# Alternating halves of up and down projections in an MoE layer, and the high part of keys and queries a round ahead of the low part, on one core

## The chip, the core and the metric

The kernel runs on one core of a Trainium2 chip. The metric is the device time of one execution in microseconds (us). The kernel before takes 898.13 us, the median of three runs (897.16 to 899.61). The profile is of one further execution, of 898.34 us.

The engines are TensorE (PE; its weight loads are PEld), VectorE (DVE), ScalarE (ACT), GpSimd (POOL) and SyncE (SP, which only issues DMAs here). Each works through its own queue of instructions in order, and waits on semaphores for the others.

## What is computed

Attention with soft-capped scores, then a first MoE layer (one expert, no routing), then a second one with a normalised gate. Tensors are float32; the weights arrive as float64.

```python
# attention: batch 4, 12 heads, 448 tokens, 64 per head
scores = cap * tanh(q @ k.T / sqrt(64) / cap)          # cap = 30
attn = softmax(scores)                                  # over the keys
x = (attn @ v)                                          # -> 1792 tokens x 768
# first MoE layer, 768 -> 2048 -> 768
h = x @ w_in
x = (h - tanh(h)) @ w_out
# second MoE layer, 768 -> 1024 -> 768
h = x @ w_in2
e = exp(h - max(h))
solu = h * e / (sum(e) + 1e-9)
out = (layernorm(solu) * g_ln) @ w_out2
```

## The kernel before

The 1792 tokens are worked on in two halves (`hb` 0 and 1), one after the other: attention, first MoE layer, second MoE layer for the first half, and then the same for the second half. A half of 896 tokens has 12 pairs of heads.

Products are computed to nearly full float32: every operand is split into a high part in the matmul's float format (`...h`) and the rest (`...l`), and one product is three matmuls, high x high, high x low and low x high. The splitting is work for VectorE and ScalarE. The float64 weights are taken apart on VectorE as well (lines L111 to L113 turn the words `st` into a float32 `f`, L120 makes the low part `w`); the second half reads most of them back as saved, split tiles.

**Attention.** The order of the work is written by hand: the loop over rounds in `attention` issues in each round one step of each of several pairs, and every engine keeps that order. `load(p)` fetches keys and queries of pair p (`kq`, three buffers, mostly by GpSimd's queue), `split_qk(p)` makes `kqh` by a cast and `kql` by a subtraction on VectorE (L290, L291, two buffers each), `scores(p)` (L308 into the PSUM tile `s`, L314 into `x`), `tanh(p)` and the exponential on ScalarE, `values(p)` (L340 into `o`), and on VectorE the sums `sm` (L362, L363) and the copies `ou` (L382) and `su` (L387), which release the PSUM buffers that `o`, `so` and `x` share.

**The tiles' memory.** SBUF tiles come from pools by stage. In the attention `kqh` and `kql` are in one pool, their buffers one behind the other. A pool of the next stage stands on memory that a pool of the stage before had, and a tile's first writer waits for the last user of that memory. So the second attention's tiles stand on those of the first half's second MoE layer, whose last output tiles `ot` (three, each 128 x 768) are copied from PSUM (L761, L763, L765) and sent to `out` by SyncE (L766).

**First MoE layer.** The 2048 hidden columns come in four chunks (`NCHUNK` = 4) of four tiles of 128. `up(c, half)` computes two hidden tiles of a chunk into the PSUM tiles `hp` (L500 to L502; tag "a", two buffers), and `nonlinear` makes g = h - tanh h of each, by ScalarE and by VectorE's L534 (`gf`), L537 (`t`), L538, L539, and splits it into `gh` and `gl` (L543; six buffers each, a chunk needs four). `down(c)` goes over the six output tiles d = 0 to 5: each is a product over the chunk's four hidden tiles into the PSUM tile `op` (L556 to L558; tag "b", two buffers), which is then added to the accumulator `acc` in SBUF (L563, VectorE; for chunk 0 a copy by ScalarE). An up or down tile has 896 columns, worked on as blocks of 512 and 384; `turned()` alternates which comes first. Here the scheduler orders each engine's instructions from the program's order and its estimates.

What decides the order around the change are these lines, in which a chunk's up tiles come before the down tiles of the chunk ahead of it:

```python
        for c in range(NCHUNK):
            if c + 1 < NCHUNK:
                up(c + 1, 0)
                up(c + 1, 1)
            down(c)
```

Of the kernel before, what the change touches and what calls it, by code (L numbers as in the profile page):

```python
# [10 lines left out]
F32R = mybir.dt.float32r  # L11
# [18 lines left out]
def fused_kernel(ctx, tc, qk_in, v, cap, w1, w2, w3, w4, gln, out):  # L30
    nc = tc.nc
    B, H, S, D = 4, 12, 448, 64
    DM = H * D
    P = 128
# [4 lines left out]
    NK = DM // P  # L39
# [6 lines left out]
    KW = qk_in.shape[3] - S  # L46
    KQ0 = KW - 128

    NCHUNK = w2.shape[0] // NK
# [31 lines left out]
    def caps(part):  # L81
        if part == 0:
            nc.vector.reciprocal(tscale, capt)
            nc.vector.tensor_scalar_mul(tscale, tscale, 1.0 / math.sqrt(D))
            return
        nc.vector.scalar_tensor_tensor(ncap, capt, -1.0, capt, ALU.mult, ALU.min)
        nc.vector.tensor_scalar(shift, ncap, 64.0, 0.0, ALU.add, ALU.min)
        nc.vector.scalar_tensor_tensor(guard, ncap, math.log(1e-9), shift, ALU.add, ALU.add)
# [117 lines left out]
    def load_w1(c, half):  # L206
        ts = []
        for i in range(NK // 2):
            ts += cols(unit(f"1_{c}_{half}_{i}", w1u[(c * 2 + half) * (NK // 2) + i], 2), 2)
        return ts  # L210
# [51 lines left out]
    def attention(ap, hb, xh, xl, rest=None):  # L262
        pairs = [(bb, j) for bb in range(HB) for j in range(NP)]
        n = len(pairs)
        raw, qk, vs, sc, ts, os_, so, fin, rss, rds, rbs, sm = ({} for _ in range(12))
# [13 lines left out]
        def load_v(p):  # L279
# [2 lines left out]
            (nc.sync if hb == 0 and p < 2 else nc.gpsimd).dma_start(vf, v[HB * hb + bb, j])  # L282
            vs[p] = vf

        def split_qk(p):
            kq = raw.pop(p)
            h = ap.tile([P, KW + S], F32R, tag="kqh", name="kqh")
            l = ap.tile([P, KW + S], F32R, tag="kql", name="kql")
            for cs in (slice(KQ0, KW + S), slice(0, KQ0)) if hb == 0 and p == 0 else (slice(0, KW + S),):
                nc.vector.tensor_copy(h[:, cs], kq[:, cs])  # L290
                nc.vector.tensor_tensor(l[:, cs], kq[:, cs], h[:, cs].bitcast(F32), ALU.subtract)  # L291
            qk[p] = (h, l)
            if hb == 0 and p == 0:
                caps(0)
            if hb == 0 and p == 1:
                caps(1)
# [133 lines left out]
        def at(p, fn, *a, m=n):  # L430
            if 0 <= p < m:
                fn(p, *a)
# [3 lines left out]
        for i in range(-5, n):  # L436
            e = i + 2
            at(i, values)
            at(i + 1, tanh)
            at(i, sums_added if hb else sums)  # L440
            at(i - 2, finish1)
            at(i - 3, finish2)
            at(i - 5, finish3)
            at(i + 3, split_qk)
            at(i, evict_v)
            if hb:
                at(i, evict_s, m=n - 1)
            at(i + 2, scores)
            at(i + 1, exp)
            if hb:  # L450
                at(i + 1, presum)
            if hb == 0 and i == 0:
                nc.scalar.activation(gcol, guard, AF.Exp)
            if rest and i == -1:
                rest[2]()
            if not hb:
                at(i, evict_s, m=n - 1)
            at(e - 2, mid, m=WA)
            at(i + 5, load)
            at(e, fetch, m=WA)  # L460
            at(i + 3, load_v)
            at(e - 3, low, m=WA)
            at(e - 1, high, m=WA)
# [16 lines left out]
    def moe1(mp, hb, xh, xl, yh, yl):  # L480
        acc = [mp.tile([P, HT], F32, tag=f"acc{d}", name=f"acc{d}", bufs=1) for d in range(NK)]
        gs = {}
        place.update(pool=(mp, WX1), at=-1)

        blocks = [(0, 512), (512, HT)]

        def turned():
            blocks.reverse()
            return list(blocks)

        def flat(ps):
            return ps.rearrange("p a b -> p (a b)")

        def up_mms(hp, wt, m, k0, k1, gg=None):
            ms = slice(m * P, (m + 1) * P)
            parts = [(flat(hp)[:, a:b], slice(a, b)) for a, b in turned()] if gg is None else [(hp[:, g, :S], slice(g * S, (g + 1) * S)) for g in gg]
            for o, cs in parts:
                for kk in range(k0, k1):
                    wh, wl = wt[kk]
                    nc.tensor.matmul(o, wh[:, ms], xh[kk][:, cs], start=(kk == 0), stop=False)  # L500
                    nc.tensor.matmul(o, wh[:, ms], xl[kk][:, cs], start=False, stop=False)  # L501
                    nc.tensor.matmul(o, wl[:, ms], xh[kk][:, cs], start=False, stop=(kk == NK - 1))  # L502

        def first():

            gs[0] = []
            wts = [load_w1(0, 0), load_w1(0, 1)]
            hps = [pst("hp", "ab"[half]) for half in range(2) for _ in range(2)]
            for g, k0, k1 in ((0, 0, NK), (1, 0, 3), (1, 3, 4), (1, 4, 5), (1, 5, 6)):
                for m in range(3):  # L510
                    up_mms(hps[m], wts[m // 2], m % 2, k0, k1, (g,))
                    if k1 == NK and g == 1:
                        nonlinear(0, hps[m])
            up_mms(hps[3], wts[1], 1, 0, NK)
            nonlinear(0, hps[3], True)

        def up(c, half):
            gs.setdefault(c, [])
            wt = load_w1(c, half)
            for m in range(2):  # L520
                hp = pst("hp", "a")
                up_mms(hp, wt, m, 0, NK)
                nonlinear(c, hp, True)

        def nonlinear(c, hp, whole=False):
            h = flat(hp)[:, :HT].rearrange("p (a b) -> p a b", a=2) if whole else hp[:, :, :S]
            u = mp.tile([P, 2, S], F32, tag="u", name="u")
            nc.scalar.activation(u, h, AF.Square)  # L528
            t = mp.tile([P, 2, S], F32, tag="t", name="t")
            nc.scalar.activation(t, h, AF.Tanh)  # L530
            mk = mp.tile([P, 2, S], U8, tag="mk", name="mk")
            nc.scalar.activation(mk, t, AF.Square, scale=TS)
            gf = mp.tile([P, 2, S], F32, tag="gf", name="gf")
            nc.vector.scalar_tensor_tensor(gf, u, C2, h, ALU.mult, ALU.mult)  # L534
            w = mp.tile([P, 2, S], F32, tag="w", name="w", bufs=1)
            nc.scalar.activation(w, u, AF.Square, bias=gat)
            nc.vector.tensor_tensor(t, h, t, ALU.subtract)  # L537
            nc.vector.scalar_tensor_tensor(gf, w, GB, gf, ALU.add, ALU.mult)  # L538
            nc.vector.copy_predicated(gf, mk, t)  # L539
            gh = mp.tile([P, 2, S], F32R, tag="gh", name="gh", bufs=6)  # L540
            gl = mp.tile([P, 2, S], F32R, tag="gl", name="gl", bufs=6)
            nc.scalar.copy(gh, gf)
            nc.vector.tensor_tensor(gl, gf, gh.bitcast(F32), ALU.subtract)  # L543
            gs[c].append((gh, gl))

        def down(c):
            for d in range(NK):
                wt = load_w2(c, d)
                op = pst("op")
                nm = CH // P  # L550
                fo = flat(op)
                for a, b in turned():
                    for m in range(nm):
                        gh, gl = (flat(g)[:, a:b] for g in gs[c][m])
                        wh, wl = wt[m]
                        nc.tensor.matmul(fo[:, a:b], wh, gh, start=(m == 0), stop=False)  # L556
                        nc.tensor.matmul(fo[:, a:b], wh, gl, start=False, stop=False)  # L557
                        nc.tensor.matmul(fo[:, a:b], wl, gh, start=False, stop=(m == nm - 1))  # L558
                a = acc[d]
                if c == 0:  # L560
                    nc.scalar.copy(a, fo[:, :HT])
                else:
                    nc.vector.tensor_tensor(a, fo[:, :HT], a, ALU.add)  # L563
                if c == NCHUNK - 1:
                    nc.scalar.copy(yh[d], a)
                    nc.vector.tensor_tensor(yl[d], a, yh[d].bitcast(F32), ALU.subtract)

        first()
        if hb:
            for _ in range(3):  # L570
                held = sp.tile([P, 512, 2], U32, tag="st", name="held", bufs=3)
                nc.vector.tensor_copy(held[:, 0, :1].bitcast(F32), flat(gs[0][3][1])[:, :1].bitcast(F32))
        for c in range(NCHUNK):
            if c + 1 < NCHUNK:
                up(c + 1, 0)
                up(c + 1, 1)
            down(c)
            if hb and c < NK // 2:
                sums_w3(c)

# [316 lines left out]
```

## Time and profile before

| | |
|---|---|
| median of three runs | 898.13 us (897.16 to 899.61) |
| profiled execution | 898.34 us |
| its span (first to last instruction) | 896.6 us |
| mean granted TensorE clock | 0.998 |
| TensorE busy | 886.3 us, 99% |
| VectorE busy | 700.7 us, 78% |
| ScalarE busy | 431.7 us, 48% |
| bytes moved | 150.83 MB |

Busy time is the time in which an engine had an instruction under way; matmuls overlap, so that a busy TensorE can still be one that is held up between two of them, or that runs at a lower clock. The granted clock says which share of TensorE's full 2.4 GHz the chip gave it in a stretch. Waits are idle times of an engine by what ended them. In a row, L500 is the kernel's line, `hp<-xh,w` the tile written and those read, and x4 the number of instructions that a row stands for.

### The profile page before, as it was taken

To read this page: it belongs to the slowest core of one execution; us is meant where nothing else is said; L and a number is where in the kernel's file an instruction comes from. 1 tells how busy PE (TensorE), PEld (TensorE's weight loads), DVE (VectorE), ACT (ScalarE), POOL (GpSimd) and SP (SyncE) were. 2 spreads that over 40 slices of the span, in tenths; PEclk is the share of its full clock that TensorE was granted. 3 is DMA by queue.
4 is the path that set the end of the run, shared out by engine and by line. 5 is a ranking of instruction groups with operands and counts; after the bars stand their busy time and mean duration, and the time that the engine had idled before them with its cause. 6 is when DMAs were issued, how large, how long until landed. Compare 5 with 4: busy or idle time off the path is not lost.

```text
span 896.6 us, 13069 instructions
## 1 busy us (share of the span) xinstructions
PE 886.3 (99%) x5135; PEld 709.5 (79%) x5135; DVE 700.7 (78%) x1071; ACT 431.7 (48%) x483; POOL 49.0 (5%) x88
## 2 busy tenths in 40 slices
PE   9999999999999999999999999999999999999998
PEld 5444699888989888888874447989899989887887
DVE  6687889989999892788437997796999874679851
ACT  7999367446154231443158990763642621222311
POOL 2211000000000000001022210000000000000100
PEclk9999999999999999999999999999999999999999
DMA  8554690675643874631155732356765542266101
GB/s 293 185 183 144 215 350 24 224 250 183 191 138 121 283 246 156 228 138 47 53 200 198 221 128 88 118 179 215 238 213 196 173 148 75 93 211 223 68 36 53
DMA packets 48584, 150.83 MB, mean 168 GB/s; under 512 B 10700, under 2 KB 13772, under 8 KB 48524
## 3 DMA queue, kind: packets, MB, share of 16 engines
q1 hardware_dynamic: 41340, 120.81, 40.4%
q0 software_dynamic: 7040, 29.20, 9.4%
q8 instruction: 40, 0.66, 0.3%
q14 instruction: 20, 0.16, 0.0%
q10 hardware_dynamic: 144, 0.00, 0.0%
HBM read 109.65 MB, written 40.19 MB: 167 GB/s over the span
## 4 chain that ended last, share of the span: by engine, by line
PE 61%; DVE 5%; DMA 1%; ACT 1%; issue 1%; SPq 0%; DVEq 0%
PE op L557 5%; PE op L558 5%; PE op L556 5%; PE hp L500 4%; PE hp L502 4%; PE hp L501 4%; PE hp L258 4%; PE hp L259 4%; PE hp L260 4%; PE oab L755 2%; PE oab L759 2%; PE oab L756 2%; PE o L340 2%; PE s L308 2%; PE tp L609 1%; PE oab L757 1%
## 5 line engine op out<-in xcount | busy, mean ns | idle before, releaser
L500 PE MATMUL hp<-xh,w 128*128 128x512 f32 (+2 forms) x384 | 140.2, 366 | 2.1 <-DVE t L537 2.1
L501 PE MATMUL hp<-xl,w 128*128 128x512 f32 (+2 forms) x384 | 140.3, 365 | 0.0
L502 PE MATMUL hp<-xh,w 128*128 128x512 f32 (+2 forms) x384 | 140.2, 365 | 0.0
L557 PE MATMUL op<-gl,w 128*128 128x512 f32 (+1 forms) x336 | 122.2, 364 | 1.1 <-DVE gl L543 1.0
L558 PE MATMUL op<-gh,w 128*128 128x512 f32 (+1 forms) x336 | 122.2, 364 | 0.0
L556 PE MATMUL op<-gh,w 128*128 128x512 f32 (+1 forms) x336 | 121.7, 362 | 0.0
L119 ACT CAST w<-f 128x512 fp32r<-128x512 f32 x60 | 37.3, 622 | 117.0 <-DVE f L113 95.3
L500 PEld LDWEIGHTS hp<-xh,w 128*128 128x128 f32 x384 | 72.4, 189 | 12.1 <-issue 3.7
L502 PEld LDWEIGHTS hp<-xh,w 128*128 128x128 f32 x384 | 72.5, 189 | 8.1 <-issue 0.7
L501 PEld LDWEIGHTS hp<-xl,w 128*128 128x128 f32 x384 | 72.5, 189 | 8.1 <-issue 0.7
L340 PE MATMUL o<-t,vf 128*32 128x448 f32 x768 | 77.8, 542 | 0.0
L332 ACT ACTIVATE t<-t,shift,capt 128x3136 f32<-128x3136 f32 (+2 forms) x26 | 72.8, 2807 | 0.7
L557 PEld LDWEIGHTS op<-gl,w 128*128 128x128 f32 x336 | 63.1, 188 | 9.0 <-DVE gl L543 1.9
L556 PEld LDWEIGHTS op<-gh,w 128*128 128x128 f32 x336 | 63.1, 188 | 7.1
L558 PEld LDWEIGHTS op<-gh,w 128*128 128x128 f32 x336 | 63.0, 188 | 6.5
L325 ACT ACTIVATE t<-s,tscale 128x1344 f32<-128x1344 f32 x48 | 63.5, 1380 | 5.6 <-PE s L308 5.6
L113 DVE SCALAR_TENSOR_TENSOR f<-st,f 128x512 uint32<-128x512 uint32 x90 | 61.5, 688 | 1.1
L112 DVE SCALAR_TENSOR_TENSOR f<-st,f 128x512 uint32<-128x512 uint32 x90 | 61.3, 688 | 0.9
L340 PEld LDWEIGHTS o<-t,vf 128*32 128x32 f32 x768 | 22.7, 109 | 43.4 <-issue 38.7
L563 DVE TENSOR_TENSOR acc<-op,acc 128x896 f32<-128x896 f32 x36 | 39.1, 1087 | 19.7 <-PE op L558 19.7
L528 ACT ACTIVATE u<-hp 128x896 f32<-128x896 f32 x32 | 29.5, 921 | 50.8 <-PE hp L502 50.8
L259 PE MATMUL hp<-w,xh 128*128 128x512 f32 x123 | 48.0, 390 | 0.0
(184 smaller groups left out, 1815.6 us busy)
## 6 DMA issues: line engine op xcount, KB each, us to landing
st<-in_moe_w_out_dram SPq DMA_DIRECT2D x53, 512.0 KB
d<-w SPq DMA_DIRECT2D x53, 512.0 KB
w<-d SPq DMA_DIRECT2D x37, 512.0 KB
st<-in_moe_w_in_dram SPq DMA_DIRECT2D x25, 512.0 KB
kq<-in_qk_dram POOLq DMA_DIRECT2D x21, 480.0 KB, 4.1
w<-d POOLq DMA_DIRECT2D x13, 512.0 KB, 4.9
rw<-d SPq DMA_DIRECT2D x12, 512.0 KB
dT<-tw SPq DMA_DIRECT2D x12, 512.0 KB
```

Of the source, the lines that this page charges most:

```text
L112: nc.vector.scalar_tensor_tensor(f, st[:, :, 1], 0xC0000000, f, ALU.bitwise_and, ALU.bitwise_or)
L113: nc.vector.scalar_tensor_tensor(f, st[:, :, 0], 29, f, ALU.logical_shift_right, ALU.bitwise_or)
L259: nc.tensor.matmul(ps, sh, ml, start=False, stop=False)
L325: nc.scalar.activation(t[:, 3 * half:3 * half + 3], s[half][:, :, :S], AF.Tanh, scale=tscale)
L332: nc.scalar.activation(t[:, sl], t[:, sl], AF.Exp, bias=shift, scale=capt)
L340: nc.tensor.matmul(o[cs, :S], vf[:, r, cs], t[:, 6 if r == 3 else 2 * r + g // 2], start=(r == 0), stop=(r == 3))
L500: nc.tensor.matmul(o, wh[:, ms], xh[kk][:, cs], start=(kk == 0), stop=False)
L501: nc.tensor.matmul(o, wh[:, ms], xl[kk][:, cs], start=False, stop=False)
L502: nc.tensor.matmul(o, wl[:, ms], xh[kk][:, cs], start=False, stop=(kk == NK - 1))
L556: nc.tensor.matmul(fo[:, a:b], wh, gh, start=(m == 0), stop=False)
L557: nc.tensor.matmul(fo[:, a:b], wh, gl, start=False, stop=False)
L558: nc.tensor.matmul(fo[:, a:b], wl, gh, start=False, stop=(m == nm - 1))
```

## The change

Three things are moved; no operation is added or left out.

- **Up and down alternate.** For chunks 1 and 2 the order is now: first half of the next chunk's up tiles, three down tiles of this chunk, second half of the up tiles, the other three down tiles. Chunk 0 and the last chunk keep their order. It holds for both token halves.
- **Two down tiles go over the hidden tiles outermost.** In the last down tile of chunk 2 and the first of chunk 3, the loop over the four hidden tiles is the outer one and the two column blocks the inner one; before, a column block was finished before the next.
- **The high part a round ahead.** In the second attention, `kqh` of a pair is cast one round before its `kql` is subtracted, behind `evict_s` (which issues `su`) in VectorE's order, and `kqh` has three buffers in place of two.

```diff
--- before.py
+++ after.py
@@ -282,12 +282,21 @@
             (nc.sync if hb == 0 and p < 2 else nc.gpsimd).dma_start(vf, v[HB * hb + bb, j])
             vs[p] = vf
 
+        highs = {}
+
+        def high_qk(p):
+            h = highs[p] = ap.tile([P, KW + S], F32R, tag="kqh", name="kqh", bufs=3 if hb else 2)
+            if hb:
+                nc.vector.tensor_copy(h, raw[p])
+            return h
+
         def split_qk(p):
+            h = highs.pop(p) if hb else high_qk(p)
             kq = raw.pop(p)
-            h = ap.tile([P, KW + S], F32R, tag="kqh", name="kqh")
             l = ap.tile([P, KW + S], F32R, tag="kql", name="kql")
             for cs in (slice(KQ0, KW + S), slice(0, KQ0)) if hb == 0 and p == 0 else (slice(0, KW + S),):
-                nc.vector.tensor_copy(h[:, cs], kq[:, cs])
+                if not hb:
+                    nc.vector.tensor_copy(h[:, cs], kq[:, cs])
                 nc.vector.tensor_tensor(l[:, cs], kq[:, cs], h[:, cs].bitcast(F32), ALU.subtract)
             qk[p] = (h, l)
             if hb == 0 and p == 0:
@@ -445,6 +454,7 @@
             at(i, evict_v)
             if hb:
                 at(i, evict_s, m=n - 1)
+                at(i + 4, high_qk)
             at(i + 2, scores)
             at(i + 1, exp)
             if hb:
@@ -543,19 +553,22 @@
             nc.vector.tensor_tensor(gl, gf, gh.bitcast(F32), ALU.subtract)
             gs[c].append((gh, gl))
 
-        def down(c):
-            for d in range(NK):
+        def down(c, ds=range(NK)):
+            for d in ds:
                 wt = load_w2(c, d)
                 op = pst("op")
                 nm = CH // P
                 fo = flat(op)
-                for a, b in turned():
-                    for m in range(nm):
-                        gh, gl = (flat(g)[:, a:b] for g in gs[c][m])
-                        wh, wl = wt[m]
-                        nc.tensor.matmul(fo[:, a:b], wh, gh, start=(m == 0), stop=False)
-                        nc.tensor.matmul(fo[:, a:b], wh, gl, start=False, stop=False)
-                        nc.tensor.matmul(fo[:, a:b], wl, gh, start=False, stop=(m == nm - 1))
+                bl = turned()
+                parts = [(a, b, m) for a, b in bl for m in range(nm)]
+                if (c, d) in ((NCHUNK - 2, NK - 1), (NCHUNK - 1, 0)):
+                    parts = [(a, b, m) for m in range(nm) for a, b in (bl if m % 2 == 0 else bl[::-1])]
+                for a, b, m in parts:
+                    gh, gl = (flat(g)[:, a:b] for g in gs[c][m])
+                    wh, wl = wt[m]
+                    nc.tensor.matmul(fo[:, a:b], wh, gh, start=(m == 0), stop=False)
+                    nc.tensor.matmul(fo[:, a:b], wh, gl, start=False, stop=False)
+                    nc.tensor.matmul(fo[:, a:b], wl, gh, start=False, stop=(m == nm - 1))
                 a = acc[d]
                 if c == 0:
                     nc.scalar.copy(a, fo[:, :HT])
@@ -571,10 +584,13 @@
                 held = sp.tile([P, 512, 2], U32, tag="st", name="held", bufs=3)
                 nc.vector.tensor_copy(held[:, 0, :1].bitcast(F32), flat(gs[0][3][1])[:, :1].bitcast(F32))
         for c in range(NCHUNK):
-            if c + 1 < NCHUNK:
-                up(c + 1, 0)
-                up(c + 1, 1)
-            down(c)
+            for k in range(2):
+                if c + 1 < NCHUNK:
+                    up(c + 1, k)
+                if c:
+                    down(c, range(k * NK // 2, (k + 1) * NK // 2))
+            if c == 0:
+                down(c)
             if hb and c < NK // 2:
                 sums_w3(c)
```

The order of VectorE in the first half's first MoE layer, where chunk 2's up tiles meet chunk 1's down tiles. `hp_2009` and `hp_2096` are the second and third up tile of chunk 2, `f`, `st` and the `w` of L112 to L120 belong to weights that are being converted. Before:

```order
L534 SCALAR_TENSOR_TENSOR gf_2052<-u_2046,hp_2009 128x896
L113 SCALAR_TENSOR_TENSOR f_2439<-st_2437,f_2439 128x512
L537 TENSOR_TENSOR t_2048<-hp_2009,t_2048 128x896
L538 SCALAR_TENSOR_TENSOR gf_2052<-w_2054,gf_2052 128x896
L120 TENSOR_TENSOR w_2436<-f_2439,w_2436 128x512
L539 COPY_PREDICATED gf_2052<-mk_2050,t_2048 128x896
L112 SCALAR_TENSOR_TENSOR f_2558<-st_2556,f_2558 128x512
L534 SCALAR_TENSOR_TENSOR gf_2139<-u_2133,hp_2096 128x896
L543 TENSOR_TENSOR gl_2060<-gf_2052,gh_2059 128x896
L537 TENSOR_TENSOR t_2135<-hp_2096,t_2135 128x896
```

After (L544 to L553 are the old L534 to L543, and L576 is the old L563):

```order
L544 SCALAR_TENSOR_TENSOR gf_2052<-u_2046,hp_2009 128x896
L113 SCALAR_TENSOR_TENSOR f_2439<-st_2437,f_2439 128x512
L547 TENSOR_TENSOR t_2048<-hp_2009,t_2048 128x896
L548 SCALAR_TENSOR_TENSOR gf_2052<-w_2054,gf_2052 128x896
L576 TENSOR_TENSOR acc0_1283<-op_2072,acc0_1283 128x896
L549 COPY_PREDICATED gf_2052<-mk_2050,t_2048 128x896
L120 TENSOR_TENSOR w_2436<-f_2439,w_2436 128x512
L112 SCALAR_TENSOR_TENSOR f_2558<-st_2556,f_2558 128x512
L553 TENSOR_TENSOR gl_2060<-gf_2052,gh_2059 128x896
L576 TENSOR_TENSOR acc1_1284<-op_2107,acc1_1284 128x896
```

The eviction acc0 of chunk 1's first down tile now stands where the low part of a weight (L120) stood, and that low part comes two rows later; the next up tile's `gf_2139` has left this place.

VectorE's order at the start of the second attention, with what each instruction waits for in brackets (DMAHW is a queue of DMAs that SyncE issues, DMASW one of GpSimd's). Before:

```order
L290 CAST kqh_4295<-kq_4291 128x960 [waits DMASW7_49]
L291 TENSOR_TENSOR kql_4296<-kq_4291,kqh_4295 128x960 [waits DVE_49]
L290 CAST kqh_4303<-kq_4293 128x960 [waits DMASW0_49]
L291 TENSOR_TENSOR kql_4304<-kq_4293,kqh_4303 128x960 [waits DMAHW5_49,DMAHW4_49,DMAHW6_49,DVE_49,Activation_49]
L777 COPY otz_4247<-ob_4327 128x256 [waits PE_49]
L290 CAST kqh_4392<-kq_4299 128x960 [waits DMASW1_49,PE_49]
L291 TENSOR_TENSOR kql_4393<-kq_4299,kqh_4392 128x960 [waits DVE_49]
```

After (L300 is the old L291, L793 the old L777):

```order
L290 CAST kqh_4293<-kq_4291 128x960 [waits DMASW7_49]
L300 TENSOR_TENSOR kql_4297<-kq_4291,kqh_4293 128x960 [waits DMAHW5_49,DMAHW4_49,DMAHW6_49,DVE_49,Activation_49]
L290 CAST kqh_4299<-kq_4295 128x960 [waits DMASW0_49]
L300 TENSOR_TENSOR kql_4305<-kq_4295,kqh_4299 128x960 [waits DVE_49]
L290 CAST kqh_4307<-kq_4301 128x960 [waits DMASW1_49]
L793 COPY otz_4247<-ob_4329 128x256 [waits PE_49]
L300 TENSOR_TENSOR kql_4394<-kq_4301,kqh_4307 128x960 [waits DVE_49,PE_49]
```

The third `kqh` comes ahead of its `kql`, and the wait for three DMA queues and ScalarE, which stood on the second `kql`, stands on the first.

VectorE's order in the middle of the second attention, one round. Before:

```order
L291 TENSOR_TENSOR kql_4762<-kq_4644,kqh_4761 128x960
L382 COPY ou_4765<-o_4728 128x448
L387 COPY su_4767<-so_4749 97x448
L362 TENSOR_TENSOR sm_4797<-t_4745 128x896
L363 TENSOR_TENSOR sm_4797<-sm_4797,t_4745 128x896
L394 SCALAR_TENSOR_TENSOR rs_4691<-rs_4691,gcol_82 56x16
L395 RECIPROCAL rs_4691<-rs_4691 56x16
L419 TENSOR_TENSOR ou_4463<-ou_4463,rb_4680 128x448
```

After (L391 is the old L382, L396 the old L387):

```order
L391 COPY ou_4765<-o_4730 128x448
L396 COPY su_4767<-so_4751 97x448
L290 CAST kqh_4772<-kq_4724 128x960
L371 TENSOR_TENSOR sm_4799<-t_4747 128x896
L372 TENSOR_TENSOR sm_4799<-sm_4799,t_4747 128x896
L403 SCALAR_TENSOR_TENSOR rs_4691<-rs_4691,gcol_82 56x16
L404 RECIPROCAL rs_4691<-rs_4691 56x16
L428 TENSOR_TENSOR ou_4463<-ou_4463,rb_4682 128x448
```

The cast `kqh`, which stood with `kql` directly ahead of `ou` in the round (as the first row here and those behind it show), stands behind `su`, for a pair one later.

## Rows read from the trace of the kernel before

**Rows 1.** the page, part 1: busy us (share of the span) x instructions

```profile
PE 886.3 (99%) x5135; PEld 709.5 (79%) x5135; DVE 700.7 (78%) x1071; ACT 431.7 (48%) x483; POOL 49.0 (5%) x88
```

**Rows 2.** TensorE's waits: line waited for: us in all, times, longest us

```profile
PE z L428 <- DVE xh L425: 2.1, 1, 2.1
PE hp L500 <- DVE t L537: 2.1, 1, 2.1
PE op L557 <- DVE gl L543: 1.0, 1, 1.0
PE hp L258 <- DVE rstd L604: 1.0, 1, 1.0
```

**Rows 3.** stretches (first MoE layer): us, busy per engine, granted clock, DMA share, GB/s

```profile
203.47:206.95 3.48, 3.48 (x8) 2.75 (x9) 3.48 (x6) 1.25 (x3) 0.00 (x0) 0.51 0.70 257
203.47:212.42 8.95, 8.95 (x36) 7.78 (x37) 8.95 (x13) 4.47 (x6) 0.00 (x0) 0.81 0.57 195
212.42:219.66 7.24, 7.24 (x37) 6.50 (x37) 7.24 (x10) 4.62 (x6) 0.00 (x0) 1.00 0.30 119
219.66:224.49 4.83, 4.83 (x26) 4.36 (x24) 4.83 (x8) 4.30 (x6) 0.00 (x0) 1.00 0.65 217
306.60:313.06 6.46, 5.39 (x25) 4.20 (x24) 6.36 (x11) 0.27 (x1) 0.00 (x0) 1.00 0.90 299
```

**Rows 4.** the same view, three rounds of the second attention

```profile
496.35:503.10 6.75, 6.75 (x65) 3.29 (x62) 5.26 (x11) 6.18 (x5) 1.62 (x4) 1.00 0.73 227
503.10:510.07 6.97, 6.83 (x66) 3.30 (x63) 6.80 (x12) 6.19 (x5) 2.04 (x4) 1.00 0.75 219
523.94:530.88 6.94, 6.80 (x67) 3.30 (x63) 6.77 (x12) 6.19 (x5) 1.64 (x3) 1.00 0.62 226
```

**Rows 5.** VectorE's timeline, start of the second attention: start, us, operation, [idle before]

```profile
445.71 1.16 DVE L291 TENSOR_TENSOR kql<-kq,kqh 128x960 fp32r<-128x960 f32 x1
...
454.64 1.16 DVE L291 TENSOR_TENSOR kql<-kq,kqh 128x960 fp32r<-128x960 f32 x1 [7.20 <-DMA out_dram<-ot]
...
460.87 1.09 DVE L362 TENSOR_TENSOR sm<-t 128x896 f32<-128x896 f32 x1 [1.98 <-ACT t L332]
```

**Rows 6.** all engines' timeline, start of the second attention

```profile
451.21 0.48 PE L308 MATMUL s<-kqh 64*128 64x448 f32 x2
...
451.52 0.38 PE L308 MATMUL s<-kql,kqh 64*128 64x448 f32 x2
...
451.80 0.38 ACT L763 COPY ot<-oab 128x256 f32<-128x256 f32 x1
...
452.20 0.33 SPq L766 DMA_DIRECT2D out_dram<-ot  x1
...
462.57 0.47 PE L308 MATMUL s<-kqh 64*128 64x448 f32 x2
```

**Rows 7.** VectorE's timeline, first MoE layer of the first half

```profile
202.24 1.08 DVE L537 TENSOR_TENSOR t<-hp,t 128x896 f32<-128x896 f32 x1
...
212.36 0.68 DVE L120 TENSOR_TENSOR w<-f,w 128x512 fp32r<-128x512 f32 x1
...
308.25 2.08 DVE L543 TENSOR_TENSOR gl<-gf,gh 128x896 fp32r<-128x896 f32 x2
```

**Rows 8.** VectorE's timeline, a slow round of the second attention

```profile
501.38 0.55 DVE L419 TENSOR_TENSOR ou<-ou,rb 128x448 f32<-128x448 f32 x1
...
502.93 0.65 DVE L290 CAST kqh<-kq 128x960 fp32r<-128x960 f32 x1
...
508.31 0.55 DVE L419 TENSOR_TENSOR ou<-ou,rb 128x448 f32<-128x448 f32 x1
```

**Rows 9.** DMA issues: out<-in, queue, count, KB each, median us to landing

```profile
kq<-in_qk_dram POOLq DMA_DIRECT2D x21, 480.0 KB, 4.1
```

**Rows 10.** stretches of the second half's MoE layer, columns as in rows 3

```profile
650.00:675.00 25.00, 25.00 (x129) 22.81 (x128) 24.83 (x34) 10.98 (x15) 0.00 (x0) 1.00 0.67 221
675.00:700.00 25.00, 25.00 (x126) 22.53 (x125) 20.69 (x30) 9.50 (x13) 0.00 (x0) 1.00 0.56 185
```

## Prediction

> **What bounds the kernel now.** I read the page's first part, then TensorE's waits, then single stretches. TensorE is busy for 886.3 of the 896.6 us of the span [rows 1], so time can be won only where it stands still, runs at the lower clock level, or has a tile stretched by waits. TensorE waits four times in the whole span [rows 2]. Two of the waits lie in the part that the diff rewrites, the first MoE layer of the first token half: 2.1 us before an up tile, for the VectorE line L537 that releases its PSUM buffer, and 1.0 us before a down tile, for the low part gl (L543). The other two are the first matmuls of the kernel (z) and one in the second layer (rstd), both outside the diff. TensorE never waits for a weight, nor in an attention's rounds.
>
> The first of the two has an after-effect. TensorE stops at 201.40 and starts again at 203.47 (2.07 us), and then the granted clock reads 0.51 of full speed, the lower level of the two (1.2 of 2.4 GHz), for 3.48 us; the up tile in which that falls takes 8.95 us against 7.24 for the next one [rows 3]. So this stop costs 2.07 + 1.71 = 3.78 us. The stop of 1.07 us inside the down tile at 306.60 left the clock at 1.00; the tile took 6.46 us against the 4.83 of an undisturbed one [rows 3].
>
> In the second attention, four rounds (503.10 to 530.88) take 6.93 to 6.97 us, against 6.75 before them [rows 4]. The profile after must be read at these places and at one more, the start of the second attention, where the first half's last output tiles still stand in SBUF.
>
> **The change, part by part.** Its matmuls, VectorE instructions and DMAs are the same in number; they are moved.
>
> *Part 1, start of the second attention.* The third buffer for the high part kqh is allocated ahead of the two of kql, so kql moves one buffer up in SBUF, and onto the memory of the first half's last output tiles (ot). The instruction order shows it: the wait for three DMA queues and for ScalarE, which stood at the second kql, stands now at the first. In the trace of before, the first kql ran at 445.71 without a wait, and the second waited 7.20 us, until 454.64, for "DMA out_dram<-ot" [rows 5]. There it cost nothing, since TensorE needed that pair's scores some 8 us later. The first kql is needed at once: TensorE ends the last projection and issues two score matmuls with kqh at 451.21, and at 451.52 the first that reads kql [rows 6]. The last ot is only copied at 451.80 and its DMA issued at 452.20 [rows 6], so the release stays at 454.64: nothing ahead of it in the queues has moved. The first kql then ends at 454.64 + 1.16 = 455.80; from the end of a VectorE instruction to a TensorE start I take 0.15, from L537 (202.24 + 1.08 = 203.32) to 203.47 [rows 3, 7]. TensorE stands from 451.52 to 455.95: **+4.43 us**. This is more than the 2.07 that brought the clock down at 201.40, so I add the same 1.71: **+1.7**. For the bounds: no clock fall, 0; the fall reaches one such stretch more, 3.4.
>
> Queued behind the waiting kql on VectorE are kqh and kql of the second pair, kqh of the third, and a short copy (otz): with 0.65 for a kqh [rows 8], 0.65 + 1.16 + 0.65 and the copy, done by about 459. Scores of the second pair began at 462.57 before [rows 6], and shift by the same 4.4. On GpSimd's queue the load of the fourth pair waits for the first kql, because it takes its raw buffer; it can't be issued before 455.80, lands 4.1 later [rows 9] at about 460, and its kqh now stands ahead of sm (L362), which ran at 460.87 before [rows 5] and will be 4.4 later in any case. So I add nothing for these. Without that cover the price would be the 0.65 of a kqh. What follows on TensorE has no idle time that could take the delay back.
>
> The Trainium skill, "DMA: Bandwidth & Descriptors", section "Anatomy of one DMA — SWDGE (gpsimd) path", gives a DMA a fixed 2.0 us or so, mostly the write receipt, plus its bytes over 436 GB/s. For the 384 KB of an ot that makes an estimate of 2.9 us after the issue, for a queue that is not the one used here; the trace has 454.64 - 452.20 = 2.44 [rows 5, 6]. By the page the stop would be about 0.5 longer and the time 903.3; the trace decides, and I leave it out.
>
> *Part 2, halves of up and down alternating, first half.* After the second up tile of chunk 2, TensorE now goes on with down tiles of chunk 1, whose inputs are ready: the 2.07 us wait for L537 and its clock fall go, **-3.78**. What is late next is the down tiles' PSUM. They have two buffers, so the third needs the eviction acc0 of the first. In VectorE's new order acc0 stands at row 289, where w (L120) stood, behind t and gf of the nonlinear; that w started at 212.36, with VectorE busy for 8.95 of the 8.95 us before it [rows 3, 7], and nothing ahead of row 289 has changed. So acc0 ends at 212.36 + 1.08 = 213.44 and TensorE can go on at 213.59. It comes to the third down tile at 201.40 + 2 x 4.83 = 211.06 (4.83 from rows 3): a wait of 2.53 and, being longer than 2.07, the clock fall again: **+2.53 + 1.71 = +4.24**. Net +0.46. Bounds: if VectorE comes early enough that the wait stays near the 1.07 which left the clock alone, down to -3.8 + 1.1 or, without any wait, -3.8; above, one more VectorE instruction of 0.68 to 1.08 ahead of acc0, +1.5. I take +0.46, since VectorE had no idle time there. The low part w moved behind acc0 and L539 is 2.2 us later; its cover is the ring of weight buffers, out of which no wait came in [rows 2].
>
> *Part 3, block order of two down tiles.* With m outermost, the last down tile of chunk 2 has done with its first two gh and gl in its first half, so that the gh and gl of chunk 3 can be written there, and the first down tile of chunk 3 needs its third and fourth gl only from its middle on. Together that is some 4.8 us of slack against the 2.08 of the two gl (308.25, [rows 7]). The tile of 6.46 becomes 4.83: **-1.63**. Bounds: 0 (they stay late because alternating moved VectorE's work here) and -1.63.
>
> *Part 4, high part a round ahead.* In the slow rounds kqh and kql stand directly before the copy ou that releases the PSUM buffer of x, and VectorE's own round (501.38 to 508.31) is 6.93, just over TensorE's 6.75 [rows 4, 8]. With kqh (0.65) moved behind ou and su, ou comes 0.65 earlier, while the round stays as long. The four rounds run up 27.78 - 4 x 6.75 = 0.78, of which 0.65 is taken: **-0.65**. Bounds: 0 and -0.78.
>
> *Part 5, the alternation in the second half.* There TensorE does not wait at all now. VectorE is busy for 24.83 of 25 us at 650, then for 20.69 of 25 [rows 10], and an eviction will now stand behind a nonlinear there as in part 2. Bounds: 0, and 2.1 + 1.7 as at 201.40. VectorE's slack just behind is 4 us in 25, so I take a low value: **+0.4**.
>
> Sum: 4.43 + 1.7 + 0.46 - 1.63 - 0.65 + 0.4 = +4.71, on the profiled execution's 898.34: 903.05. The median of the runs is 0.21 below it, so the forecast is **902.8 us**.
>
> **The rivals.**
> - *VectorE is early at the third down tile* (chance 0.13). The wait of part 2 falls under about 1.1 us and the clock holds. For it: eviction and nonlinear order are set by the scheduler, and weight words may arrive otherwise. Against: VectorE was saturated there. 902.8 - 4.24 = 898.6.
> - *The clock holds at the attention's start* (0.13). For it: the stop of 1.07 at 307 did not lower it, and one row with 0.51 is a single instance. Against: 4.43 is twice the 2.07 that did. 902.8 - 1.7 = 901.1. The Trainium skill, "TensorE: Matmul & The Clock Gate", section "What's actually happening", has the lower level as the default, which activity releases; by it alone this rival would have no chance and the sum would stay at 902.8.
> - *A full stop with clock fall in the second half's MoE layer* (0.12). For it: 24.83 of 25 us of VectorE. Against: it goes slack right after. 902.8 - 0.4 + 3.8 = 906.2.
> - *Not slower: the first kql does not stop TensorE* (0.06). The place is 451.52; the mechanism is that the release comes before 451.52 - 0.15 - 1.16 = 450.2, or that kql's memory is not that of the ot still in use. Then part 1 goes, with its clock fall: 902.8 - 6.13 = 896.7. For it: the first kql ran at 445.71 without a wait. Against: the wait now stands on it, and the ot is written only at 451.80.
>
> **How the numbers follow.** The forecast has 0.56; its own range is 901.3 to 904.4 (part 2 from -0.5 to +1, part 5 from 0 to +1). A measurement of this kernel can tell about 0.3%, 2.7 us: "the same" is 895.4 to 900.8. In it lie the first rival, most of the last, a third of the second and a few hundredths of the forecast: 0.20. Faster takes the last rival together with the first (892.5): 0.04. Slower: 0.76. The range of 8 in 10 goes from 898.5 (it leaves out the last rival and a part of the first) to 906.3 (part of the third).
>
> **What the profile after would show.** TensorE's waits: s for VectorE kql, about 4.4 us at 451; op for VectorE acc, about 2.5 us at 211; no hp for t; no op for gl at 307. The granted clock at 0.5 for some 3.5 us behind each of the two stops. VectorE's first kql behind a wait of 8 to 9 us for out_dram<-ot. Rounds of 6.75 throughout the second attention. I am wrong if the first kql runs near 445, if no wait for acc shows at 211, or if TensorE has waits over 1 us between 580 and 720.

## The result and the profile after

The changed kernel takes 902.96 us (median of five runs, 901.18 to 904.32), against 898.13 before (five runs too by now); the ratio is 1.0054, with an interval of 1.0040 to 1.0068. It is slower by about 4.8 us; the forecast was 902.8. Its profiled execution took 903.32 us, its span 901.3.

The page's first part, and TensorE's waits (line waited for: us in all, times, longest us):

```profile
PE 888.3 (99%) x5135; PEld 713.3 (79%) x5135; DVE 702.2 (78%) x1071; ACT 431.6 (48%) x483; POOL 48.9 (5%) x88
```

```profile
PE s L317 <- DVE kql L300: 4.2, 1, 4.2
PE op L569 <- DVE acc L576: 2.1, 1, 2.1
PE z L437 <- DVE xh L434: 2.1, 1, 2.1
PE hp L258 <- DVE rstd L620: 1.0, 1, 1.0
```

Against [rows 1] TensorE is busy 2 us longer, with the same number of matmuls, and the span is 4.7 longer. Against [rows 2] the waits for t (L537) and gl (L543) are gone; new are one of 4.2 us before the scores s, for the first kql, and one of 2.1 us before a down tile, for acc.

The largest is at the start of the second attention. VectorE's timeline there, to be held against [rows 5]:

```profile
443.53 0.65 DVE L290 CAST kqh<-kq 128x960 fp32r<-128x960 f32 x1
453.05 1.16 DVE L300 TENSOR_TENSOR kql<-kq,kqh 128x960 fp32r<-128x960 f32 x1 [8.87 <-DMA out_dram<-ot]
...
454.81 1.16 DVE L300 TENSOR_TENSOR kql<-kq,kqh 128x960 fp32r<-128x960 f32 x1
```

The first kql, which ran at 445.71 without a wait, now waits 8.87 us for the output tiles' DMA. The second, which had that wait, follows without one. All engines at the same place, to be held against [rows 6]:

```profile
449.62 0.47 PE L317 MATMUL s<-kqh 64*128 64x448 f32 x2
...
450.62 0.33 SPq L782 DMA_DIRECT2D out_dram<-ot  x1
...
454.26 0.74 PE L317 MATMUL s<-kql,kqh 64*128 64x448 f32 x2 [4.17 <-DVE kql L300]
```

The last output DMA is issued at 450.62 and lets the first kql go at 453.05, 2.43 us later (2.44 before). TensorE issued the two matmuls that need only kqh at 449.62, ended them 0.47 later, at 450.09, and stood until 454.26.

VectorE in the first half's MoE layer, to be held against [rows 7]:

```profile
210.14 1.10 DVE L547 TENSOR_TENSOR t<-hp,t 128x896 f32<-128x896 f32 x1
211.15 1.10 DVE L548 SCALAR_TENSOR_TENSOR gf<-w,gf 128x896 f32<-128x896 f32 x1
212.14 1.10 DVE L576 TENSOR_TENSOR acc<-op,acc 128x896 f32<-128x896 f32 x1
213.15 1.20 DVE L549 COPY_PREDICATED gf<-mk,t 128x896 f32<-128x896 uint8 x1
214.19 0.72 DVE L120 TENSOR_TENSOR w<-f,w 128x512 fp32r<-128x512 f32 x1
```

acc stands where w (L120) stood, at 212.14, behind t and gf, and w comes two places later.

Stretches (us, busy time of each engine, granted clock, DMA share, GB/s): the third down tile of chunk 1 and its piece at the lower clock, the first down tile of chunk 3, the 6 us behind the attention's stop, two rounds of the attention, three down tiles of the second half:

```profile
213.29:219.85 6.56, 6.55 (x25) 5.69 (x25) 6.56 (x10) 1.56 (x2) 0.00 (x0) 0.74 0.34 110
214.60:218.10 3.50, 3.50 (x11) 2.85 (x10) 3.50 (x6) 0.72 (x1) 0.00 (x0) 0.51 0.37 150
306.74:311.58 4.84, 4.84 (x26) 4.35 (x25) 4.84 (x8) 0.09 (x1) 0.00 (x0) 1.00 0.89 313
454.26:460.27 6.01, 6.00 (x28) 5.19 (x29) 2.25 (x3) 2.65 (x2) 3.14 (x6) 0.50 0.75 255
508.55:515.29 6.74, 6.74 (x65) 3.38 (x62) 6.60 (x12) 6.18 (x5) 2.01 (x4) 1.00 0.70 202
528.76:535.49 6.73, 6.73 (x65) 3.29 (x61) 6.41 (x12) 6.18 (x5) 1.26 (x3) 1.00 0.75 233
649.04:663.87 14.83, 14.81 (x74) 12.97 (x72) 14.66 (x19) 6.44 (x8) 0.00 (x0) 1.00 0.40 153
```

The down tile at 213.29 takes 6.56 us where an undisturbed one takes 4.83 [rows 3], with 3.50 us at 0.51 in it; the tile at 306.74 takes 4.84, and took 6.46 [rows 3]. Behind the attention's stop the clock is at 0.50 for 6.01 us. The rounds that took 6.94 to 6.97 [rows 4] take 6.73 and 6.74.

TensorE's starts in the two traces give the balance by stage (the stages' ends are the first matmuls of the next):

| stage | before | after | difference |
|---|---|---|---|
| first half, chunks 1 to 3 of the first MoE layer | 150.47 | 149.01 | -1.46 |
| first half, second MoE layer | 113.97 | 113.75 | -0.22 |
| second attention, first scores to second scores | 11.36 | 18.51 | +7.15 |
| second attention, the ten rounds behind | 68.30 | 67.36 | -0.94 |
| second half, first MoE layer | 230.10 | 230.38 | +0.28 |

The sum is 4.81; the spans differ by 4.7.

### The profile page after: what moved, and what is told of

Its sections match the earlier page's. It is cut to its first block, busy times and chain, and to the rows that moved or that the text cites. A ratio compares the mean times of both kernels' runs of the same rounds, so it can differ in the third digit from the quotient of the medians.

```text
span 901.3 us, 13068 instructions
## 1 busy us (share of the span) xinstructions
PE 888.3 (99%) x5135; PEld 713.3 (79%) x5135; DVE 702.2 (78%) x1071; ACT 431.6 (48%) x483; POOL 48.9 (5%) x88
## 4 chain that ended last, share of the span: by engine, by line
PE 88%; DVE 7%; DMA 2%; ACT 2%; issue 1%; DVEq 0%; ACTq 0%
PE o L349 8%; PE op L569 7%; PE op L571 7%; PE op L570 7%; PE hp L512 7%; PE hp L511 7%; PE hp L510 7%; PE s L317 5%; PE hp L258 4%; PE hp L259 4%; PE hp L260 4%; PE oab L771 2%; PE oab L775 2%; PE oab L772 2%; PE x L323 2%; PE so L366 2%
## 5 line engine op out<-in xcount | busy, mean ns | idle before, releaser
L112 DVE SCALAR_TENSOR_TENSOR f<-st,f 128x512 uint32<-128x512 uint32 x90 | 61.0, 685 | 0.9
L576 DVE TENSOR_TENSOR acc<-op,acc 128x896 f32<-128x896 f32 x36 | 39.0, 1084 | 15.3 <-PE op L571 15.2
```

What stands on the lines that cost most here:

```text
L112: nc.vector.scalar_tensor_tensor(f, st[:, :, 1], 0xC0000000, f, ALU.bitwise_and, ALU.bitwise_or)
```

## Experiments

Each ratio is to the kernel before, measured on the same chip, with its 95% interval. The first four kernels ran on one chip (the kernel before: 898.10 us, 21 runs), the last four on another (897.40, 29 runs), so that across these groups, and against the changed kernel's 902.96, ratios are compared and not medians. Waits and stretches are those of one profiled execution each.

**The two halves of the change, apart.** The changed kernel with `split_qk` and the round as they were, and the other way round, with the MoE layer's loops as they were:

```diff
 # the attention part undone, against the changed kernel
-            h = highs.pop(p) if hb else high_qk(p)
             kq = raw.pop(p)
+            h = ap.tile([P, KW + S], F32R, tag="kqh", name="kqh")
...
-                at(i + 4, high_qk)
 # the MoE part undone, against the changed kernel
-                if (c, d) in ((NCHUNK - 2, NK - 1), (NCHUNK - 1, 0)):
-                    parts = [(a, b, m) for m in range(nm) for a, b in (bl if m % 2 == 0 else bl[::-1])]
...
-            for k in range(2):
...
+            if c + 1 < NCHUNK:
+                up(c + 1, 0)
+                up(c + 1, 1)
+            down(c)
```

> The changed kernel with the attention part undone: only the MoE layer's alternation and the two down tiles with the hidden tiles outermost. Theory (all of the loss is made at the start of the second attention): the MoE parts give -1.46 us in the first half and +0.28 in the second, as the two traces show between the same tiles, so 898.1 - 1.2 = 896.9. Rival (the alternation is what costs): at or above 902. The op line should still wait some 2.1 us for acc at 211, and the clock should fall behind it.

> Only the attention part of the change, the MoE layer as before. Theory: the first round of the second attention is 7.15 us longer (18.51 against 11.36) and the ten rounds behind it together 0.96 shorter: 898.1 + 6.2 = 904.3. Rival (the loss sits in the MoE layer): 898.1 - 1.0 = 897.1.

The MoE part alone: 897.91 us, ratio 0.9996 (0.9987 to 1.0005), no difference that can be told. The attention part alone: 904.12 us, ratio 1.0076 (1.0062 to 1.0090). So the loss is made in the attention, as the theory had it, and the MoE part, by its interval, gives back at most about its 1.2 us. TensorE's waits that differ, of the first, then of the second, and the second's stretches behind the attention's stop (columns as above):

```profile
PE op L559 <- DVE acc L566: 2.9, 1, 2.9
```

```profile
PE s L317 <- DVE kql L300: 4.2, 1, 4.2
...
PE hp L510 <- DVE t L547: 1.7, 2, 1.0
PE op L568 <- DVE gl L553: 1.3, 1, 1.3
```

```profile
455.30:458.00 2.70, 2.68 (x16) 2.01 (x16) 2.27 (x3) 0.94 (x1) 2.34 (x4) 0.63 0.42 114
458.00:460.30 2.30, 2.30 (x15) 2.23 (x14) 0.00 (x0) 1.71 (x2) 0.40 (x2) 0.70 0.99 399
```

In this execution of the first, the wait for acc is 2.9, in the changed kernel's 2.1. In the second, whose MoE layer is that of before, the wait for t is two of at most 1.0 us, where [rows 2] have one of 2.1. So the stops there come out differently from one execution to the next, and the profile of before was a dear one in that stage. The clocks of the other executions say the same: the profile of before, with one fall of the clock, has a mean granted clock of 0.998, and of the 50 runs of the same kernel beside the experiments 47 have 0.999 or 1.000. With the MoE part alone, 7 of 11 have 0.998 or less.

**The third buffer alone.**

```diff
-            h = ap.tile([P, KW + S], F32R, tag="kqh", name="kqh")
+            h = ap.tile([P, KW + S], F32R, tag="kqh", name="kqh", bufs=3 if hb else 2)
```

> The kernel before with nothing but a third buffer for kqh in the second attention; the casts stay where they were. Theory (the place of the buffers in SBUF makes the wait, not the order of the casts): the first kql waits for the last output tiles' DMAs, TensorE stops about 4.2 us and runs at the lower clock behind it, +7.15: 905.3. The four rounds of 6.94 stay. Rival (the cast issued a round ahead makes the stop): no stop, 898.1.

Measured 904.70 us, ratio 1.0079 (1.0066 to 1.0092). No instruction is moved here, and still the first kql waits (VectorE's timeline) and TensorE with it (its waits), with a low clock behind (the stretch):

```profile
443.48 0.65 DVE L290 CAST kqh<-kq 128x960 fp32r<-128x960 f32 x1
453.10 1.16 DVE L291 TENSOR_TENSOR kql<-kq,kqh 128x960 fp32r<-128x960 f32 x1 [8.97 <-DMA out_dram<-ot]
```

```profile
PE s L308 <- DVE kql L291: 4.2, 1, 4.2
...
PE x L314 <- DVE ou L382: 0.9, 4, 0.3
```

```profile
454.30:460.30 6.00, 5.99 (x30) 5.20 (x31) 1.69 (x2) 2.65 (x2) 2.73 (x5) 0.53 0.73 252
```

The place of the buffers makes the stop. The lone buffer also shows what moving the cast is worth: without it the wait of x for ou stays, four times 0.3 at most, and the last four rounds take 7.00 to 7.06 us.

**kql's buffers ahead of kqh's.**

```diff
-        with pools(f"a{hb}", ("t",), ("kqh", "kql"), ("ou",), ("rb", "rs", "su"), None) as ap, banks(f"pa{hb}", ("s", 2), ("o", 2)):
+        with pools(f"a{hb}", ("t",), ("kql",), ("kqh",), ("ou",), ("rb", "rs", "su"), None) as ap, banks(f"pa{hb}", ("s", 2), ("o", 2)):
```

> The changed kernel with one edit: kql and kqh get a pool each, kql's ahead, so that the two kql lie where nothing waits for the output tiles, and the second and third kqh lie on those tiles. Theory: the first kql runs at about 445, TensorE does not stop at the attention's start, the wait of some 8 us stands on the second kqh, where it has cover until the second pair's scores 11 us later: 903.0 - 7.15 = 895.8. Rival (the wait only changes its tile and still reaches TensorE, at the second pair's scores): 899 to 903.

Measured 897.03 us, ratio 0.9994 (0.9984 to 1.0004), where the changed kernel has 1.0054: one line takes back about 5.4 us. VectorE's timeline, TensorE's waits, and two stretches (the third down tile of chunk 1, and the first attention round):

```profile
444.94 1.16 DVE L300 TENSOR_TENSOR kql<-kq,kqh 128x960 fp32r<-128x960 f32 x1
453.86 0.66 DVE L290 CAST kqh<-kq 128x960 fp32r<-128x960 f32 x1 [7.77 <-DMA out_dram<-ot]
```

```profile
PE op L569 <- DVE acc L576: 3.3, 2, 2.1
...
PE oa L258 <- DVE otz L793: 0.5, 1, 0.5
```

```profile
213.69:218.69 5.00, 5.00 (x25) 4.46 (x26) 5.00 (x7) 1.12 (x2) 0.00 (x0) 1.00 0.26 106
450.44:462.38 11.94, 11.49 (x71) 9.40 (x70) 6.54 (x8) 7.32 (x7) 2.72 (x5) 1.00 0.59 215
```

The first kql runs at 444.94 as before; the wait for the output tiles, 7.77, stands on the second kqh. The rival, that it still reaches TensorE, is right by a little: the copy otz is behind it on VectorE's queue, TensorE waits 0.5 for otz, and the first round takes 11.94 against 11.36. That is 0.6 of the 1.2 (1.8 by the ratio) by which it misses the expected 895.8; where the rest lies is not shown.

**Something for TensorE to do during the stop.** The changed kernel with the narrow part of the last projection issued before the first scores:

```diff
             s = [psum["s"].tile([P, 3, 512], F32, tag="s", name="s") for _ in range(2)]
+            narrow, wide, evict = rest if rest and p == 0 else (None, None, None)
+            if narrow:
+                narrow(psum["o"].tile([P, 512], F32, tag="o", name="ob"))
...
-            narrow, wide, evict = rest if rest and p == 0 else (None, None, None)
-            if narrow:
-                narrow(psum["o"].tile([P, 512], F32, tag="o", name="ob"))
```

> The changed kernel with one edit: at the second attention's start TensorE does the narrow part of the last projection (some 30 matmuls into ob, 3 us at the full clock) before the first scores, not after them. The first kql waits as long as in the changed kernel. Theory (the loss is idle TensorE and the clock behind it): the stop of 4.2 shrinks to about 1.2, which did not bring the clock down at 307, so some 3.0 of the stop and some 2.9 of the clock come back: 903.0 - 5.9 = 897.1. If the clock falls all the same: 900. Rival (another wait, not the first kql, holds the stage): 903.

Measured 898.24 us, ratio 1.0003 (0.9993 to 1.0013); 897.1 was expected. TensorE's waits, and the stretches of the narrow part and of the round behind it:

```profile
PE op L569 <- DVE acc L576: 2.5, 2, 1.9
...
PE ob L258 <- ACT ot L779: 0.9, 1, 0.9
```

```profile
450.55:453.61 3.06, 3.06 (x24) 2.93 (x24) 0.65 (x1) 0.00 (x0) 0.00 (x0) 1.00 0.32 129
453.61:462.47 8.86, 8.77 (x46) 6.52 (x45) 5.54 (x8) 6.35 (x5) 4.88 (x8) 1.00 0.77 268
```

The stop is down to 0.9 us, before ob and for the copy of ot, and in this execution the clock is at 1.00 in both stretches. The first kql waits 8.96 us as ever; that wait costs only by what TensorE lacks meanwhile. Narrow part and round take 11.92 us together, 6.6 less than the changed kernel's 18.51 and more than the 5.9 expected to come back, so the miss of 1.1 (1.3 by the ratio) does not lie here. Seven of the twelve runs have a mean granted clock of 0.998, so the clock fell somewhere in them; where is not shown.

**Alternation and loop order, apart.** The kernel before with only the first, and with only the second:

```diff
 # alternation alone, against the kernel before
...
-            if c + 1 < NCHUNK:
-                up(c + 1, 0)
-                up(c + 1, 1)
-            down(c)
+            for k in range(2):
+                if c + 1 < NCHUNK:
+                    up(c + 1, k)
+                if c:
+                    down(c, range(k * NK // 2, (k + 1) * NK // 2))
+            if c == 0:
+                down(c)
 # loop order alone, against the kernel before
...
+                if (c, d) in ((NCHUNK - 2, NK - 1), (NCHUNK - 1, 0)):
+                    parts = [(a, b, m) for m in range(nm) for a, b in (bl if m % 2 == 0 else bl[::-1])]
```

> The kernel before with the alternation alone: no hidden tiles outermost, attention as before. Theory: the wait for t before an up tile goes and one of 2 to 3 us for acc before the third down tile of chunk 1 comes, with or without the lower clock; the first down tile of chunk 3 still waits about 1 us for gl, since its gl can only be written when the last down tile of chunk 2 is done with both blocks: 898 to 899. Rival (alternation already ends the gl wait, and the loop order of the two tiles does nothing): as the MoE parts together, 897.9.

> The kernel before with the two down tiles over the hidden tiles outermost, and nothing else. Theory: no wait for gl, the tile at 306 takes 4.84 in place of 6.46, the stop for t before an up tile stays: 898.1 - 1.6 = 896.5. Rival (VectorE sets the pace of this stage, the time is waited elsewhere): 898.1.

Alternation alone: 898.66 us, ratio 1.0009 (0.9997 to 1.0021). Loop order alone: 896.38 us, ratio 0.9989 (0.9978 to 0.9999). TensorE's waits with alternation alone, and those in the MoE layers with loop order alone:

```profile
PE op L557 <- DVE acc L564: 2.6, 3, 1.6
...
PE op L558 <- DVE gl L543: 1.0, 1, 1.0
```

```profile
PE hp L500 <- DVE t L537: 2.0, 3, 1.1
PE hp L500 <- issue: 1.6, 1, 1.6
```

With alternation alone the gl wait is there, so the rival falls; with the loop order it is gone, whatever the rest. The gain of that is small, about 1 us, and only just clear of none. The profiled execution of that kernel was its slowest (898.37) and shows one more stop, of 1.6 us before an up tile of the second half; the profile names no releaser for it. It ends 0.1 us after a t on VectorE (642.69 + 1.08 = 643.77, TensorE at 643.87), so it is probably one more wait for t; that is not shown. Alternation by itself gains nothing; at best its interval reaches 0.3 us of gain. It trades the wait for t for one for acc.

**A version that avoids both.** The changed kernel with kql's buffers ahead and with two down tiles before the second half of the up tiles and four behind:

```diff
-                    down(c, range(k * NK // 2, (k + 1) * NK // 2))
+                    down(c, range(2) if k == 0 else range(2, NK))
-        with pools(f"a{hb}", ("t",), ("kqh", "kql"), ("ou",), ("rb", "rs", "su"), None) as ap, banks(f"pa{hb}", ("s", 2), ("o", 2)):
+        with pools(f"a{hb}", ("t",), ("kql",), ("kqh",), ("ou",), ("rb", "rs", "su"), None) as ap, banks(f"pa{hb}", ("s", 2), ("o", 2)):
```

> The changed kernel with two edits: kql's pool ahead of kqh's, and the down tiles of chunks 1 and 2 shared out two and four around the second half of the up tiles, in place of three and three. Theory: two down tiles have a PSUM buffer each, so none waits for the eviction acc while VectorE is behind with the nonlinear; neither stop, t nor acc, shows in the first half: the 897.0 of the changed kernel with kql ahead, less 2.1 to 3.9: 893 to 895. Rival (VectorE is behind in this stage whatever the order, and the stop comes at another tile): 897.

Measured 893.97 us (six runs, 893.06 to 894.16), ratio 0.9958 (0.9944 to 0.9972), faster than both kernels; the mean granted clock is 0.999 or 1.000 in all six. All its TensorE waits over 0.2 us:

```profile
PE z L437 <- DVE xh L434: 2.1, 1, 2.1
PE hp L258 <- DVE rstd L620: 1.0, 1, 1.0
PE oa L258 <- DVE otz L793: 0.6, 1, 0.6
PE op L569 <- DVE acc L576: 0.3, 1, 0.3
```

Two down tiles fit into the two PSUM buffers, so none waits for acc while VectorE is at the nonlinear; of both stops 0.3 us is left. Against the 0.9994 with three and three that is about 3.2 us, in the range of 2.1 to 3.9 expected.

## Why the prediction was right, and which terms were off

- **Part 1, the stop.** Right in place, cause and size: 4.17 us of wait where 4.43 was forecast, release 2.43 after the DMA's issue. The 0.15 from VectorE's end to TensorE's start was too much: kql ends at 453.05 + 1.16 = 454.21, and TensorE starts at 454.26. The rest of the 0.26 is that the wait counts from the end of the two matmuls before it, at 450.09, 0.47 after their start, where I had 0.31. The third buffer alone and kql's pool ahead show the cause from both sides.
- **Part 1, the clock.** The mis-sized term. I had +1.7, from the one stretch of 3.48 us at 203.47; here the stretch at half clock was 6.01 us long, so that some 3.0 were lost. The first round measures the whole: +7.15, of which 4.17 is the stop. With the third buffer alone it was 6.92 longer (18.28), with the attention part alone 5.93 (17.28): the term lies between about 1.8 and 3.0. The rival that the clock holds there did not come in any of the three.
- **Part 2.** The mechanism was right: acc at VectorE's old place of w, a wait of 2.14 for the 2.53 forecast, a tile 1.73 longer for the 1.71. What was wrong is the size of what goes: the 3.78 was read from one execution, and the same code in two other executions (the kernel with the attention part alone, and with the third buffer alone) stops 1.7 and 1.9 in two pieces, and takes 31.08 and 31.40 us for the four up tiles where the profile of before has 32.89. Only three of those 50 runs of the kernel before have a mean clock as low as the profile's 0.998, so the 1.71 of the clock's part was not a usual cost. The profiled execution as a whole, at 898.34, is still close to the median of 898.13; where the others lose that time is not shown. Against the dear execution alternation came out at +0.07 (61.89 to 61.96 us from chunk 2's up tiles to chunk 3's) where +0.46 was forecast; timed by itself, at 1.0009, it is no gain and perhaps a cost.
- **Part 3.** Right: 4.84 for the tile, no wait for gl, and -1.53 between the same tiles (88.58 to 87.05 from chunk 3's up tiles to the layer's end); -1.0 in the timed runs of the loop order alone.
- **Part 4.** Right in mechanism: -0.94 for -0.65. All rounds come to 6.72 to 6.75, so the whole excess of 0.78 goes, and a little of the ordinary round with it.
- **Part 5.** +0.28 for +0.4. In the trace after it is the one group of three down tiles at 649 that takes 14.83 where the next takes 14.51; in the trace of the MoE part alone that group takes 14.49. The rival of a full stop there did not come.

The total, +4.98 between the two profiled executions for +4.71 forecast, is nearer than its terms, and that is luck: their errors cancel. The clock's term was 1.3 too small. Against it, the stop came out 0.26 lower, part 2 0.4 lower, and parts 4 and 5 with the second layer, for which nothing was forecast, 0.6 lower together. The forecast's own range does not follow from the values given for it: part 2 from -0.5 to +1 and part 5 from 0 to +1 make 901.4 to 903.9, not 901.3 to 904.4. The measured 902.96 lies in both.

## What to carry to other kernels

In pools laid out as here, a buffer more is also a shift of every tile allocated behind it: look up which tile of the stage before lies under each first-used tile, and put the tile that is needed last onto the memory that comes free last. When a wait is removed, follow the engine that was late: if it is as busy as before, its next product is late, here the eviction for the third of two buffers, and the order that helps is the one that asks of it what it has already done. A stop's price read from one execution, the clock's part above all, is one sample.

## What the runs showed that I had not expected

Stops of about 2 us brought the clock down in one kernel's execution and not in another's: behind 2.07 (before), 2.14 (after) and 2.88 us (the MoE part alone) the granted clock read 0.50 to 0.51 for over 3 us, behind 2.15 us in the kernel with kql ahead it stayed at 1.00, and the tile took 5.00 us. The same MoE part gave a mean clock of 0.998 or less in 7 of 11 executions of the one kernel and in 2 of 11 of the other. Behind the attention's stop of 4.2 us the clock fell in the profiled executions of all three kernels that have it, for about 6 us in two of them (0.50 and 0.53 over 6.0 us) and for less in the third (0.63 and 0.70 over two stretches of 5.0 us together).
